# A recurrent attention block and a mixture of experts on one core: the value products of one sequence ahead of those of the other

## The chip, the core and the metric

The kernel runs on one core of a Trainium2 chip. A core has a matrix engine (TensorE, "PE" in the profile, with its weight loads as "PEld"), three engines for element-wise work (VectorE "DVE", ScalarE "ACT", GpSimd "POOL"), a queue for transfers (SyncE, "SP") and 16 DMA engines. Each engine works through its own queue in order, and engines wait for one another by semaphores. TensorE writes its products into PSUM, a memory of eight banks, from which VectorE and ScalarE read. The metric is the device time in microseconds of one execution, as the median of several.

## The reference

Two blocks follow one another. The first is a gated linear recurrence over 768 steps for 4 sequences with 8 heads of width 48; the second sends each of the 3072 rows to one of 16 experts, chosen in two levels.

```python
f = 1.0 / (1.0 + np.exp(-f_logit))                    # (B, H, S, D) = (4, 8, 768, 48)
for t in range(S):
    state = f[:, :, t, :, None] * state + np.einsum('bhd,bhe->bhde', k[:, :, t], v[:, :, t])
    y[:, :, t] = np.einsum('bhd,bhde->bhe', q[:, :, t], state)
x = np.ascontiguousarray(y.transpose(0, 2, 1, 3)).reshape(B * S, H * D)     # (3072, 384)
...
g_idx = np.argmax(x @ w_group, axis=1)                # one of 4 groups
for g in range(4):
    xg = x[g_idx == g]
    e_idx = np.argmax(xg @ w_expert[g], axis=1)       # one of 4 experts of the group
    for e in range(4):
        h = np.maximum(xg[mask_e] @ w1[g, e], 0.0)    # (rows, 1024)
        out[tok_idx] = combined[:, None] * (h @ w2[g, e])
```

`combined` is the product of the two softmax weights of the chosen group and expert.

## The kernel before

**Units.** The recurrence is computed in chunks of 128 steps. There are 6 chunks `c` and 2 pairs `s` of sequences, so 12 units, numbered 0 to 11, with `units[i] = (c, s)`. A unit holds 128 steps of two sequences (`b` = 0 and 1) with 8 heads each; heads are taken two by two, as `a` (0 to 3) and `r` or `h` (0, 1).

**Within a chunk** the result is a product of masked scores with the values, plus a product of the state before the chunk with the queries. A unit passes through these steps, each a generator that an order advances from one `yield` to the next:

- `bounded` (`c`, line 581, VectorE) and `gated` (`g`, lines 591 to 607): the gate's logarithm (Exp and Ln on ScalarE), its sums over the steps (line 600, TensorE), and two exponentials into `eq` and `kh` (ScalarE).
- `multiplied` (`m`, lines 620 and 623, VectorE) and `turned` (`t`, lines 634 and 635): queries and keys are scaled and then transposed into `Tq` and `Tk`.
- `scored` (`s`): for each `b` 16 products on TensorE (line 660) write scores into two banks `ap`, one for each `r`; VectorE multiplies both with the triangle `tri` and leaves the masked scores in `am[b][:, r]` (line 663). So there are four such mask instructions in a unit, in the order (b=0, r=0), (0, 1), (1, 0), (1, 1).
- `weighed` (`w`): two banks `ys[0]` and `ys[1]`, one for each sequence. The first step adds the products with the old state (line 698, left out in chunk 0), the second the products of the values with the masked scores (line 702), 16 of them with 64 columns of weights. `CORNERS` is `[(0, 0), (0, 1), (1, 0), (1, 1)]`, pairs of `b` and `h`: the head within the pair is `b ^ h`, and `h` says which half of the bank's partitions is written. Then ScalarE copies each bank into `xT[:, b]` (line 705).
- `stated` (`n`, lines 677 to 686): the next state, left out in the last chunk, and with it its 16 products (line 677).
- `done` (`d`): the router's logits from `xT` (line 718), turned by line 723 and summed by line 724. After the second pair of a chunk the chunk's routing (`routed`, `r`) is put in line.
- `listed` (`x`): `xT` is transposed back into rows (line 743), copied by ScalarE (lines 745 and 748), and the rows are kept (units 0 to 7, sent later by SP, line 759) or written to `x_dram` at once (line 751, from POOL in units 8 and 9, from ScalarE's queue in 10 and 11).
- `decayed` (`b`, lines 644 and 645): the chunk's decay.

Each product of 32-bit numbers is two records in the profile, one for each of its two passes, except for transposes, which are one.

**What sets the order.** The order on TensorE, VectorE, ScalarE and SP is the order in which the program issues the instructions; only POOL's is left to the planner. It is written out by hand as lists of steps; a number behind a letter is an offset to the unit:

```python
EVEN = "l+2 d-2 n-1 r r r x-1 x-1 t t t t g+1 g+1 x-1 r s s s s c+2 w d-1 g+2 w g+2 n m+1 m+1".split()
ODD = "l+2 d-2 r r x-1 x-1 t t t t b n-1 g+1 g+1 x-1 r s s s s c+2 w d-1 g+2 w g+2 n m+1 m+1 r n".split()
```

So TensorE's queue around the change is, unit by unit: scores (660), old state (698), logits of the unit before (718), **values with masked scores (702)**, next state (677), logits of an earlier unit turned (723), rows (743), transposes (634), gate sums (600). VectorE's is: four masks (663), bound (581), scaling (620, 623), then routing. ScalarE's is: logits copied (720), Exp (591), the two copies to `xT` (705), Ln (594), rows (745, 748), transposes (635). Units 0 to 2 have an order of their own (`BEGIN`), where `w1 w1` of unit 1 is followed by `d0 x1 x1`; so have the last three.

**Routing.** `route` (lines 178 to 256) finds each row's expert and its place there, and writes weight and number of the row as `meta` to `x_dram` (line 246, POOL). When chunk 3 (`CLOSE`) has been counted, `load_early` ranks the experts on VectorE (lines 271 to 289) and SP starts to load the weights of the two largest (line 381). When its routing ends, `choose_early` names their first 128 rows each (line 318), and `early` gathers these from `x_dram` (line 393, POOL, tile `xg` by `rows_e`), transposes them (line 429), and runs both expert layers (lines 439 and 460) between the last steps of the recurrence; the steps of `early` are the `e` in

```python
NU: "d-2 r e d-1 x-1 x-1 d-1 x-1 r r r e e r e r r e r r e r e r r e e e e e".split(),
```

**Experts.** After the recurrence, passes over the 16 experts follow: a gather of rows (393), the first layer (439) with Relu (440), the second layer (475 or 460), a transpose, the row's weight, and a scatter into the output (450). Weights are loaded by SP three passes ahead.

Of the kernel before, what the change touches and what calls it, by code (L numbers as in the profile page):

```python
# [23 lines left out]
def kernel(  # L24
# [21 lines left out]
    HP = H // 2  # L46
# [33 lines left out]
    def bank(shape, name):  # L80
        return ps.tile(shape, FP32, tag="bank", name=name)
# [437 lines left out]
    with ExitStack() as fast:  # L519
# [29 lines left out]
        CORNERS = [(b, h) for b in range(2) for h in range(2)]  # L549
# [139 lines left out]
        def weighed(i):  # L689

            c, s = units[i]
            w = live[i]
            ys = [bank([P, HP, P], f"y{b}") for b in range(2)]
            if c:
                for a in range(HP):
                    for b, h in CORNERS:
                        rows = slice(DP * (b ^ h), DP * (b ^ h) + D)
                        nc.tensor.matmul(ys[b][DP * h:DP * h + DP, a, :], lhsT=states[s][c % 2][rows, b, a, :], rhs=w["Tq"][rows, b, a, :], start=(a == 0), stop=False, skip_group_check=True)  # L698
            yield
            for a in range(HP):  # L700
                for b, h in CORNERS:
                    nc.tensor.matmul(ys[b][DP * h:DP * h + DP, a, :], lhsT=w["v"][:, b, 2 * a + (b ^ h), :], rhs=w["am"][b][:, b ^ h, a, :], start=(c == 0 and a == 0), stop=True, skip_group_check=True)  # L702
            w["xT"] = xT = sb.tile([P, 2, HP, P], FP32, tag="xT", name="xT")
            for b in range(2):
                nc.scalar.copy(xT[:, b], ys[b])  # L705
            yield
# [73 lines left out]
        def advance(gens):  # L780
# [6 lines left out]


        STAGES = {"c": bounded, "g": gated, "m": multiplied, "t": turned, "s": scored, "n": stated, "w": weighed, "d": done, "x": listed, "b": decayed}
        BEGIN = """c0 h g0 p g0 g0 m0 m0 m0 m0 l2 t0 t0 t0 t0 c1 g1 g1 s0 s0 s0 s0 g1 g1 p w0 w0 n0 m1 m1 m1 m1 l3 h x0 x0 x0  # L790
            t1 t1 t1 t1 b1 c2 g2 g2 s1 s1 s1 s1 p d0 g2 g2 n0 n1 w1 w1 m2 m2 l4 n1
# [274 lines left out]
```

## Time and profile before

| | us |
|---|---|
| median of 5 runs | 418.03 (417.65 to 418.88) |
| the profiled execution | 418.04 |
| its span, first instruction to last | 416.2 |
| TensorE busy | 404.4 (97% of the span) |
| weight loads busy | 375.1 |
| VectorE busy | 267.1 |
| ScalarE busy | 157.3 |
| POOL busy | 83.2 |
| line 702's matmuls, 384 records | 25.1 |
| line 663's masks, 48 instructions | 29.8 |
| line 705's copies, 24 instructions | 12.9 |

The recurrence fills the first 140 us of the span, the experts the rest. The first bursts of line 702 in the 12 units start at 15.01, 25.87, 35.97, 46.96, 57.53, 68.62, 79.19, 90.28, 100.84, 111.95, 124.02 and 133.19 us.

How the profile's lines are read. In the page's second part the span is cut into 40 slices of 10.4 us, and a digit is the busy share in tenths (9 is 90% or more). A line of a group gives line number, engine, operation, output and inputs, shapes and count, then busy time in us, the mean of one in ns, and the engine's idle time just before with what ended it. A line of the timeline gives start and length in us, engine, line, operation, names, shapes and the count of instructions merged into it; in brackets stands the idle time before it, and what ended it. Matmuls are pipelined and their ends are modelled, so a record is longer than the distance to the next.

### The profile page before, as it was taken

To read this page: it belongs to the slowest core of one execution; us is meant where nothing else is said; L and a number is where in the kernel's file an instruction comes from. 1 tells how busy PE (TensorE), PEld (TensorE's weight loads), DVE (VectorE), ACT (ScalarE), POOL (GpSimd) and SP (SyncE) were. 2 spreads that over 40 slices of the span, in tenths; PEclk is the share of its full clock that TensorE was granted. 3 is DMA by queue.
4 is the path that set the end of the run, shared out by engine and by line. 5 is a ranking of instruction groups with operands and counts; after the bars stand their busy time and mean duration, and the time that the engine had idled before them with its cause. 6 is when DMAs were issued, how large, how long until landed. Compare 5 with 4: busy or idle time off the path is not lost.

```text
span 416.2 us, 10080 instructions
## 1 busy us (share of the span) xinstructions
PE 404.4 (97%) x4055; PEld 375.1 (90%) x4055; DVE 267.1 (64%) x778; ACT 157.3 (38%) x353; POOL 83.2 (20%) x127
## 2 busy tenths in 40 slices
PE   5999999999999999999999999999999999999995
PEld 3888888888788878989999999999999999999992
DVE  5666787878898731540799777495595595594240
ACT  5777766666564421211122121232231231231220
POOL 4000010101012047001041321311322321120230
PEclk9999999999999999999999999999999999999999
DMA  9999976778999639985729477495595695595010
GB/s 173 211 194 221 194 151 138 150 149 154 268 332 393 229 131 354 384 289 206 253 100 324 132 261 248 158 331 186 195 349 145 243 330 191 200 321 162 28 47 24
DMA packets 132121, 88.98 MB, mean 214 GB/s; under 512 B 102630, under 2 KB 122700, under 8 KB 132066
## 3 DMA queue, kind: packets, MB, share of 16 engines
q1 hardware_dynamic: 125666, 75.50, 61.8%
q0 software_dynamic: 5792, 11.92, 9.3%
q10 hardware_dynamic: 608, 0.83, 0.6%
q8 instruction: 34, 0.56, 0.6%
q14 instruction: 21, 0.17, 0.1%
HBM read 78.71 MB, written 9.83 MB: 213 GB/s over the span
## 4 chain that ended last, share of the span: by engine, by line
PE 48%; issue 29%; DMA 9%; POOL 6%; DVE 3%; ACT 2%; POOLq 1%
PE hp L439 12%; DMA out_dram<-yt,xg 7%; PE yo L475 6%; PE y L702 5%; PE ap L660 4%; PE cs L600 4%; PE yo L460 4%; POOL out_dram L450 4%; POOL xg L393 2%; PE x_ps L743 2%; PE tr_q L634 2%; PE ds L677 2%; PE tr_k L634 2%; DMA xg<-x_dram,rows_e 2%; PE y L698 2%
## 5 line engine op out<-in xcount | busy, mean ns | idle before, releaser
L439 PE MATMUL hp<-xe,w 128*128 128x128 f32 (+14 forms) x864 | 138.6, 320 | 0.0
L439 PEld LDWEIGHTS hp<-xe,w 128*128 128x128 f32 x864 | 135.8, 190 | 0.8
L475 PE MATMUL yo<-h,w 128*128 128x230 f32 (+13 forms) x672 | 115.8, 333 | 0.0
L422 DVE STREAM_TRANSPOSE yr<-yT 32x192 f32<-32x192 f32 (+1 forms) x208 | 70.5, 339 | 70.4 <-ACT yT L476 67.8
L475 PEld LDWEIGHTS yo<-h,w 128*128 128x128 f32 x672 | 113.7, 190 | 0.2
L415 DVE STREAM_TRANSPOSE xe<-xg 32x192 f32<-32x192 f32 (+1 forms) x208 | 69.7, 335 | 8.6 <-PE hp L439 5.6
L440 ACT ACTIVATE h<-hp 128x256 f32<-128x256 f32 (+14 forms) x72 | 34.4, 478 | 103.5 <-PE hp L439 103.5
L450 POOL DMA_INDIRECT out_dram<-yt,xg x32 | 34.4, 1075 | 149.1 <-ACT yt L447 143.6
L476 ACT COPY yT<-yo 128x230 f32<-128x230 f32 (+13 forms) x42 | 13.5, 326 | 80.5 <-PE yo L475 80.5
L393 POOL DMA_INDIRECT xg<-x_dram,rows_p x30 | 29.6, 988 | 52.7 <-DMA out_dram<-yt,xg 30.0
L663 DVE TENSOR_TENSOR am<-ap,tri 128x512 f32<-128x512 f32 x48 | 29.8, 683 | 12.2 <-PE ap L660 12.2
L702 PE MATMUL y<-am,v 128*64 128x128 f32 x384 | 25.1, 278 | 0.8 <-DVE am L663 0.8
L702 PEld LDWEIGHTS y<-am,v 128*64 128x64 f32 x384 | 20.9, 136 | 4.7 <-DVE am L663 1.9
L660 PE MATMUL ap<-Tq,Tk 48*64 48x128 f32 x768 | 23.8, 272 | 0.2 <-ACT Tk L635 0.2
L660 PEld LDWEIGHTS ap<-Tq,Tk 48*64 48x64 f32 x768 | 20.8, 133 | 2.1 <-issue 1.1
L460 PE MATMUL yo<-w,h 128*128 128x384 f32 x64 | 21.3, 486 | 0.0
L600 PE MATMUL cs<-ld_f,tri 128*128 128x384 f32 x48 | 19.7, 536 | 0.7 <-ACT ld_f L594 0.6
L460 PEld LDWEIGHTS yo<-w,h 128*128 128x128 f32 x64 | 11.9, 190 | 7.4
L607 POOL DMA_DIRECT2D ends<-eq x10 | 5.4, 542 | 57.0 <-ACT eq L601 57.0
L447 ACT ACTIVATE yt<-yr,xg 128x384 f32<-128x384 f32 (+13 forms) x26 | 14.4, 604 | 5.4 <-DVE yr L422 5.4
L705 ACT COPY xT<-y 128x512 f32<-128x512 f32 x24 | 12.9, 589 | 8.6 <-PE y L702 8.6
L634 PE MATMUL tr_q<-ident,qh 128*128 128x128 f32 x96 | 14.9, 278 | 0.3 <-DVE qh L620 0.3
(171 smaller groups left out, 366.3 us busy)
## 6 DMA issues: line engine op xcount, KB each, us to landing
w<-in_moe_w_dram SPq DMA_DIRECT2D x34, 1536.0 KB, 10.8
qh<-in_q_dram SPq DMA_DIRECT2D x12, 384.0 KB, 5.1
ld_k<-in_k_dram SPq DMA_DIRECT2D x12, 384.0 KB, 6.0
v<-in_v_dram SPq DMA_DIRECT2D x12, 384.0 KB, 5.6
ld_f<-in_f_logit_dram SPq DMA_DIRECT2D x11, 384.0 KB, 5.5
x_dram<-x_kept SPq DMA_DIRECT2D x2, 1536.0 KB, 10.9
x_dram<-x POOLq DMA_DIRECT2D x2, 384.0 KB, 7.4
x_dram<-x ACTq DMA_DIRECT2D x2, 384.0 KB, 8.3
```

What stands on the lines that cost most here:

```text
L393: nc.gpsimd.indirect_dma_start(out=w["x"][:, j, :], out_offset=None, in_=x_dram[0:1 + top, :], in_offset=bass.IndirectOffsetOnAxis(ap=rows ...
L415: squares(w, lambda n, k_, rk, g, rg: nc.vector.transpose(out=xT[rg, 0:n, k_], in_=x[rk, 0:n, g]))
L422: squares(w, lambda n, k_, rk, g, rg: nc.vector.transpose(out=y[rk, 0:n, g], in_=yT[rg, 0:n, k_]))
L439: nc.tensor.matmul(hp[:, o, :], lhsT=w1[:, ko, (f + o) * P:(f + o + 1) * P], rhs=w["xT"][:, ko, :], start=(ko == 0), stop=(ko == KO - 1))
L440: nc.scalar.activation(h[:, f:f + 2, :], hp, AF.Relu)
L450: sent = nc.gpsimd.indirect_dma_start(out=out, out_offset=bass.IndirectOffsetOnAxis(ap=w["x"][0:m, j, DM + 1:RW].bitcast(U32), axis=0), in ...
L460: nc.tensor.matmul(yp, lhsT=w["h"][:, fo, :], rhs=w2[:, fo, :], start=(fo == 0), stop=(fo == FO - 1))
L475: nc.tensor.matmul(yp, lhsT=w2[:, fo, m * P:(m + 1) * P], rhs=w["h"][:, fo, :], start=(fo == 0), stop=(fo == FO - 1))
L600: nc.tensor.matmul(cs.rearrange("t h d -> t (h d)"), lhsT=tri, rhs=nl[:, b], start=True, stop=True)
L634: nc.tensor.transpose(out=pt[:, a, :], in_=w[nm + "h"][:, b, 2 * a:2 * a + 2, :].rearrange("t r d -> t (r d)"), identity=ident)
L660: nc.tensor.matmul(ap[r][half, a, :], lhsT=w["Tk"][rows, b, a, half], rhs=w["Tq"][rows, b, a, :], start=True, stop=True)
L702: nc.tensor.matmul(ys[b][DP * h:DP * h + DP, a, :], lhsT=w["v"][:, b, 2 * a + (b ^ h), :], rhs=w["am"][b][:, b ^ h, a, :], start=(c == 0 a ...
```

## The change

Within the second step of `weighed` the 16 products of values with masked scores are issued in another order. Before, the loop over the head pairs `a` is outside and the four corners (sequence `b`, half `h`) are inside, so that products of both sequences alternate by twos. After, the loop over `b` is outside: the eight products of the first sequence come first, then the eight of the second. Within a sequence the order of `a` and `h` is as before, and so are operands, outputs, flags and the number of instructions.

```diff
             yield
-            for a in range(HP):
-                for b, h in CORNERS:
+            for b in range(2):
+                for a, h in [(a, h) for a in range(HP) for h in range(2)]:
                     nc.tensor.matmul(ys[b][DP * h:DP * h + DP, a, :], lhsT=w["v"][:, b, 2 * a + (b ^ h), :], rhs=w["am"][b][:, b ^ h, a, :], start=(c == 0 and a == 0), stop=True, skip_group_check=True)
             w["xT"] = xT = sb.tile([P, 2, HP, P], FP32, tag="xT", name="xT")
             for b in range(2):
                 nc.scalar.copy(xT[:, b], ys[b])
```

The loop over the old state in the step before (line 698) keeps its order.

## The prediction

> **What bounds the kernel.** I read the page's row of slices first, then the groups of line 702, then the timeline around each of its twelve bursts, and last the work that ends the wait at 136 us.
>
> ```profile
> PE   5999999999999999999999999999999999999995
> DMA  9999976778999639985729477495595695595010
> ...
> L702 PE MATMUL y<-am,v 128*64 128x128 f32 x384 | 25.1, 278 | 0.8 <-DVE am L663 0.8
> L702 PEld LDWEIGHTS y<-am,v 128*64 128x64 f32 x384 | 20.9, 136 | 4.7 <-DVE am L663 1.9
> ```
>
> TensorE is busy in every slice but the first and the last, so a microsecond that it loses anywhere between is a microsecond of the end, unless something else is later still. Line 702 shows only 0.8 us of idle time. But the end of a matmul is modelled, and a matmul's record (278 ns) outlasts the step to the next one, so short halts hide in "busy". They show as the length of a burst of 32 (each of the 16 products of a unit is two records):
>
> ```profile
> 35.97 1.97 PE L702 MATMUL y<-am,v 128*64 128x128 f32 x32
> 46.96 2.07 PE L702 MATMUL y<-am,v 128*64 128x128 f32 x32
> 90.28 2.07 PE L702 MATMUL y<-am,v 128*64 128x128 f32 x32
> ...
> 89.87 0.68 DVE L663 TENSOR_TENSOR am<-ap,tri 128x512 f32<-128x512 f32 x1
> ```
>
> The bursts of units 0 and 2 last 1.97, that of unit 1 1.93; those of units 3 to 8 and 10 last 2.07 each, unit 11's 2.22. The fourth mask of unit 7 ends at 89.87 + 0.68 = 90.55, 0.27 after its burst began; in the old order the third product already needs it. So seven units lose 0.10 us each there. Unit 9 loses far more:
>
> ```profile
> 107.61 0.56 DVE L684 TENSOR_TENSOR st<-sp,decays 128x384 f32<-128x384 f32 x1 [1.15 <-ACT decays L645]
> ...
> 110.99 2.46 DVE L663 TENSOR_TENSOR am<-ap,tri 128x512 f32<-128x512 f32 x4
> ...
> 111.95 0.80 PE L702 MATMUL y<-am,v 128*64 128x128 f32 x4
> 113.51 1.75 PE L702 MATMUL y<-am,v 128*64 128x128 f32 x28 [0.76 <-DVE am L663]
> ```
>
> Here VectorE is late, since it ranks the experts (lines 271 to 289) ahead of the masks: four records run, then 28 wait for the mask that ends at 113.45.
>
> A second cost of the old order is on ScalarE. Both banks fill together, so both copies of line 705 start when the whole burst is over, and where no states follow (units 1, 10 and 11) the transposes of line 743 wait for them:
>
> ```profile
> 27.63 1.07 ACT L705 COPY xT<-y 128x512 f32<-128x512 f32 x2 [1.63 <-PE y L702]
> 27.73 0.33 PE L723 MATMUL lg<-ident,lgT 128*128 128x128 f32 x1
> 28.27 1.14 PE L743 MATMUL x_ps<-ident,xT 128*128 128x128 f32 x8 [0.21 <-ACT xT L705]
> ...
> 82.11 0.33 PE L723 MATMUL lg<-ident,lgT 128*128 128x128 f32 x1
> 82.27 1.04 PE L743 MATMUL x_ps<-ident,xT 128*128 128x128 f32 x8
> ...
> 126.56 1.15 PE L743 MATMUL x_ps<-ident,xT 128*128 128x128 f32 x8 [0.21 <-ACT xT L705]
> ```
>
> At 82 us (unit 6, with line 677's work between) the same steps need 0.16 us from line 723 to line 743, and 1.04 for the eight. At 27.73 it is 0.54 and 1.14.
>
> **The change, part by part.** It adds and removes no instruction, no DMA and no tile. It reorders 16 products in TensorE's own queue; the orders of ScalarE, VectorE and SP stay as written, and nothing moves past SP's or POOL's issues. Sums are against the profiled execution: 418.04 us, a span of 416.2 and 1.8 around it. The median of the five runs is 418.03, so they are one.
>
> (a) *Masks of the second sequence are needed later.* Eight products of the first come ahead: half of 1.97 less the last record's tail of 0.27, so some 0.9 us after the burst's start (an estimate). The fourth mask is there after 0.27, some 0.6 to spare. Units 3 to 8 and 10 fall to unit 2's 1.97: 0.10 each, 0.60 by unit 8. Unit 11's 2.22 is left as it is, since its masks end at 133.12, before its burst at 133.19; a gain there would go into (e) anyhow.
>
> (b) *Unit 9.* Its 12 remaining records of the first sequence run while the last masks are made, and only 16 stay behind 113.51. At (1.75 - 0.27) / 27 = 0.055 from one to the next, the burst ends 12 x 0.055 = 0.65 sooner against VectorE.
>
> (c) *The first copy of line 705 starts about 0.9 us sooner*, and the second at the burst's end. Where ScalarE idles (1.63 ahead of 27.63, 1.50 ahead of 125.92) the transposes no longer wait: unit 1 gains 0.54 - 0.16 = 0.38 and 1.14 - 1.04 = 0.10, together 0.47 with the third digits; unit 10 likewise 0.48. The second copy ends at 27.63 + 0.59 = 28.22, and the fifth transpose would want it at 27.89 + 0.44 = 28.33, so the cover is 0.1 us; if that is gone, 0.1 of each gain is. Elsewhere the first copy still queues behind the Exp of line 591 and the transposes come after line 677's 1.09 us, so it brings nothing.
>
> (d) *One more handing-over per unit* (ScalarE is released at the 16th record too). Line 743 hands its first bank over after four of eight: 1.04 for eight and 0.60 for the four of line 634 at 83.14, (1.04 - 0.60) / 4 = 0.11 a step, and 0.11 within the four as well ((0.60 - 0.27) / 3). I take nothing. The Trainium skill, TensorE: Matmul & The Clock Gate, "The cost: per-tile semaphore tail", speaks against the change here: it counts 26.3 ns for each further increment that matmuls make. By it 12 units would pay 0.32 us, and the forecast would be 416.9; the steps of line 743 show no such cost.
>
> (e) *What is late next.* Loads don't hold it: the keys whose issue begins at 31.98 land a median 6.0 us later and are first used at 48.48. So TensorE, ScalarE and VectorE move by 0.47 + 0.60 = 1.07 up to unit 9, TensorE by 1.72 behind it, and by 1.72 + 0.10 + 0.48 = 2.30 at line 723 of 135.35. But there it must wait for a gather:
>
> ```profile
> 118.18 0.73 POOL L751 DMA_DIRECT2D x_dram<-x  x1 [11.59 <-ACT x L748]
> 120.90 0.76 POOL L246 DMA_DIRECT2D x_dram<-meta  x1 [1.80 <-DVE number L293]
> 128.99 1.06 POOL L393 DMA_INDIRECT xg<-x_dram,rows_e  x1 [7.33 <-DVE full L304]
> ...
> 135.35 0.33 PE L723 MATMUL lg<-ident,lgT 128*128 128x128 f32 x1
> 136.12 0.52 PE L429 MATMUL xg_ps<-ident,xg 128*128 128x128 f32 x3 [0.44 <-DMA xg<-x_dram,rows_e]
> ```
>
> Line 304 had ended at 128.84, but POOL's own queue shows it waiting on transfers until 128.17: the meta write of 120.90, which took 7.2 us to land, behind the x write of 118.18 in POOL's queue. The meta write follows VectorE, which has no idle time but 0.17 us from 107.6 to 122, so its issue moves by 1.07 only; the x write follows unit 9's transposes and moves by 1.72. The landing moves by something between. I take the middle, 1.4. The gather and line 429 follow it, TensorE waits 0.9 us more there, and all behind (hp, yo, the passes' gathers, the last scatter) hangs on TensorE or on routing that starts after line 429: 1.4 is what is left at the end. Sum: 418.04 - 1.4 = 416.6; bounds 418.04 - 1.72 = 416.3 and 418.04 - 1.07 = 417.0.
>
> **The rivals.**
>
> *The gather doesn't move.* The DMA row is at 9 from 104 to 135 us, and the x write of line 751 takes 5.1 us to land at best and 9.8 at worst. If bulk traffic sets the landing, all 2.3 us go into the wait at 136.12, and it is 418.0. Against it: the bulk (kept rows, expert weights) is issued behind the same engines and starts 1.07 sooner.
>
> *More gets through.* Without the x write just ahead of it the meta write needs less than 7.2 us, and the gather less than 7.0. To pass TensorE's whole 2.30 both together must lose 1.2: 415.7. For it: the largest of the x writes' times is in this very crush. Against: nothing leaves it.
>
> *Slower: runs into one bank.* Eight pairs in a row now write one bank, where the bank changed after every two. That is 3 more successions a sequence, 72 in all. If each costs the 0.10 that a halt costs now, it is 7.2 - 1.4 = 5.8 us more, 423.8. It decides from 1.4 / 72 = 0.02 us each. Against it: line 677 puts 32 records of the same shape of weights into the one bank of ds in 1.09 us, (1.09 - 0.22) / 31 = 0.028 a record, and line 718 16 into lT in 0.64. For it: neither has 128 columns to a record and two column groups at once, as line 702 does.
>
> **How the numbers follow.** Forecast 0.61, the gather stays 0.14, more gets through 0.11, slower 0.14. Its own range is 416.3 to 417.0. From 415.8 to 418.0 it takes in most of the second rival and, with a little scatter, most of the first; the slower case and what is left of these two is 2 in 10. A difference of 0.2% (0.84 us) is about what a measurement of this kernel can tell from none. The forecast and the second rival lie beyond it: 0.72 faster, 0.14 same, 0.14 slower.
>
> **What would show it.** In the profile after: bursts of line 702 at 1.97 in units 3 to 8 and 10; unit 9's idle time for am inside the burst down from 1.0 us to under 0.5; the first copy of line 705 in units 1 and 10 some 0.9 us ahead of the second, and line 743 without idle time; unit 8's burst at about 99.9 (100.84 - 0.47 - 5 x 0.10) in place of 100.84; line 429's wait for the gather up from 0.44 to over 1 us. I am wrong if bursts stay at 2.07, if they grow past it, or if line 429 starts as late as 136.1.

## The result, and the profile after

| | before | after |
|---|---|---|
| median, us | 418.29 (417.65 to 419.73, 60 runs) | 417.70 (416.39 to 418.66, 36 runs) |
| ratio to before, 95% interval | | 0.9985 [0.998, 0.999] |
| the profiled execution, its span | 418.04, 416.2 | 416.21, 414.4 |

The change gains 0.6 us, where 1.4 was forecast. The profiled execution of after is no typical one: at 416.21 us it is below all 36 timed runs. What it shows up to unit 10 recurs in other executions of this kernel, but for single halts; a line 429 as early as in it does not, and the experiments are about this difference.

The page's slices and groups of line 702 after:

```profile
PE   5999999999999999999999999999999999999995
DMA  9999997877999559984828467586496595585010
...
L702 PE MATMUL y<-am,v 128*64 128x128 f32 x384 | 24.4, 276 | 0.1
L702 PEld LDWEIGHTS y<-am,v 128*64 128x64 f32 x384 | 21.0, 137 | 3.2 <-issue 1.8
```

The group lost 0.7 us of "busy" and its 0.8 us of idle time for `am`. The timeline of after shows where, in units 2, 3, 7 and 9:

```profile
35.63 1.97 PE L702 MATMUL y<-am,v 128*64 128x128 f32 x32
46.62 1.97 PE L702 MATMUL y<-am,v 128*64 128x128 f32 x32
89.51 1.97 PE L702 MATMUL y<-am,v 128*64 128x128 f32 x32
...
110.01 2.46 DVE L663 TENSOR_TENSOR am<-ap,tri 128x512 f32<-128x512 f32 x4
...
110.97 2.65 PE L702 MATMUL y<-am,v 128*64 128x128 f32 x32
...
118.09 0.29 PE L251 MATMUL tb<-val,ln 128*128 128x64 bf16 x4 [0.67 <-DVE val L233]
```

Bursts are 1.97 in units 3 to 8 and 10, as they were in units 0 and 2. Unit 9's burst is one of 2.65 where it took from 111.95 to 115.26. The wait in the last line is new. Before, line 251 started without idle time:

```profile
119.07 0.29 PE L251 MATMUL tb<-val,ln 128*128 128x64 bf16 x4
```

Now TensorE has gained 0.65 us on VectorE in unit 9, and waits 0.67 for it at line 251.

Units 1 and 10, and the road to line 429, in the same timeline of after:

```profile
26.90 0.58 ACT L705 COPY xT<-y 128x512 f32<-128x512 f32 x1 [0.97 <-PE y L702]
27.77 0.58 ACT L705 COPY xT<-y 128x512 f32<-128x512 f32 x1 [0.29 <-PE y L702]
27.66 0.33 PE L723 MATMUL lg<-ident,lgT 128*128 128x128 f32 x1
27.82 1.25 PE L743 MATMUL x_ps<-ident,xT 128*128 128x128 f32 x8
...
116.62 0.73 POOL L751 DMA_DIRECT2D x_dram<-x  x1 [11.01 <-ACT x L748]
119.92 0.76 POOL L246 DMA_DIRECT2D x_dram<-meta  x1 [2.37 <-DVE number L293]
127.04 1.06 POOL L393 DMA_INDIRECT xg<-x_dram,rows_e  x1 [6.37 <-DVE oh L195]
...
133.93 0.33 PE L723 MATMUL lg<-ident,lgT 128*128 128x128 f32 x1
134.11 0.52 PE L429 MATMUL xg_ps<-ident,xg 128*128 128x128 f32 x3
```

Line 743 now starts 0.16 after line 723, as forecast, but its eight take 1.25 where they took 1.14 (1.04 was forecast): the second copy starts at 27.77, and the fifth transpose waits for it. And line 429 starts at 134.11 without any idle time, 2.01 us sooner than before. Forecast was a wait of over 1 us. In this execution the meta write landed after 6.27 us (7.23 before), so TensorE and the gather met.

From burst to burst, after against before: unit 1 gives 0.27 (10.10 to 9.84); units 3 to 8 give 0.10 to 0.12 each, 0.64 together; unit 9 gives 0.65 and loses it again at line 251; unit 10 gives 0.37 (9.17 to 8.80), 0.10 of it in its burst; unit 11's burst gives 0.06. That is 1.34, and with a first burst 0.08 sooner 1.42 at line 723, of the 2.30 forecast.

### The profile page after: what moved, and what is told of

It reads as the page before. It is cut to its first block, busy times and chain, and to the rows that moved or that the text cites. A ratio compares the mean times of both kernels' runs of the same rounds, so it can differ in the third digit from the quotient of the medians.

```text
span 414.4 us, 10083 instructions
## 1 busy us (share of the span) xinstructions
PE 403.2 (97%) x4055; PEld 375.2 (91%) x4055; DVE 267.0 (64%) x778; ACT 156.8 (38%) x353; POOL 83.2 (20%) x127
## 4 chain that ended last, share of the span: by engine, by line
PE 50%; issue 29%; DMA 7%; POOL 6%; DVE 3%; ACT 2%; POOLq 1%
PE hp L439 12%; DMA out_dram<-yt,xg 7%; PE yo L475 7%; PE y L702 5%; PE ap L660 5%; PE cs L600 4%; PE yo L460 4%; POOL out_dram L450 4%; PE x_ps L743 2%; POOL xg L393 2%; PE tr_q L634 2%; PE ds L677 2%; PE tr_k L634 2%; PE y L698 2%; PE lT L718 2%
```

## The experiments

Two explanations of the missing microsecond were set against one another. In the first, the **gather** (called G in the later expectations), line 429 starts when its rows land, whenever TensorE is ready. In the second, **halts** (F), TensorE stands still for parts of a microsecond inside its bursts, waiting for nothing that the trace names, while its own instructions are being fetched.

The experiments ran on four chips, the kernel before beside them on each. On three its median is 424.7 to 425.0, on the one of the wide scores below 419.08. So a run is compared with runs on its own chip, and the kernel before was also run again under names of its own (`old` and so on). Such a repeat came out at 1.0000, 0.9987 and 0.9983 of the kernel before, so that a difference of less than some 0.2% between two runs says little. The 0.15% of the result is itself no larger. The ratios are not exactly quotients of the medians given beside them; the two can differ by 0.1%.

### Both kernels again, and line 429 later

`again` is the changed kernel and `old` the kernel before, unchanged. In `late_new` and `late_old` the first `e` of the step order, line 429 with its wait, is moved behind line 743; they stand on the new and on the old order of products.

```diff
-            NU: "d-2 r e d-1 x-1 x-1 d-1 x-1 r r r e e r e r r e r r e r e r r e e e e e".split(),
+            NU: "d-2 r d-1 x-1 x-1 d-1 x-1 r e r r e e r e r r e r r e r e r r e e e e e".split(),
```

> The changed kernel, nothing else edited, for a second trace and a second timing. The profiled execution of the change had a span 1.8 us under that of before, while its median is only 0.6 us under. Theory A (the gather of the early experts' rows lands when the transfers let it): the bursts of line 702 start where they did in the first trace, unit 10's at 123.0 to 123.1 us, and the difference in span between the two traces, 1.0 us or more if this execution is a usual one, arises at the first transposes of line 429, which start between 134.1 and 135.8. Theory B (the gain is lost elsewhere: at the start, or in the experts' passes): line 429 starts at 134.1 as before and the difference arises ahead of 120 us or behind 160 us. Ratio near 0.9985 in both.

> The kernel before, nothing edited: how far two timings and two traces of one kernel differ. Ratio 1.000 within 0.001. Theory A: bursts of line 702 at the same times as in its first trace within 0.1 us, unit 10's at 124.0; line 429's first transposes anywhere between 135.4 (no wait) and 136.8. Theory B: the traces differ ahead of 120 us or behind 160 us by as much as the times do.

> The changed order with the first early expert's transposes (line 429) moved behind the last unit's rows (line 743), so that TensorE has some 1.5 us of other work before it needs the gather. Theory A: the wait for the gather goes or shrinks to the rest, and against before the time falls by 1.5 to 2.3 us (ratio 0.9945 to 0.9965), well under the changed kernel's 0.9985. Theory B: no more than 0.2 us below the changed kernel, ratio 0.998 to 0.999.

> The old order of line 702 with the same move of line 429. In the old order TensorE waits 0.4 to 0.7 us for the gather. Theory A: 0.3 to 0.7 us faster than before (ratio 0.9983 to 0.9993), and the distance from this to the changed order with the move is 1.2 us or more. Theory B: the distance between the two with the move is the same 0.6 us as without it.

Measured: `again` 424.10 us, 0.9987 [0.9965, 1.001]; `old` 424.42, 1.0 [0.9977, 1.0022]; `late_new` 424.63, 1.0003 [0.998, 1.0026]; `late_old` 424.49, 0.9995 [0.9968, 1.0023]. The first explanation had expected 0.9945 to 0.9965 for `late_new`, which lies outside its interval. Otherwise times tell nothing apart here. The traces do: from the first burst to unit 10's it is 109.04 (`old`) and 109.02 (`late_old`) in the old order, 108.10 in `late_new`, and 108.94 in `again`, which has a halt of 0.83 inside unit 6's burst. Work put ahead of the wait did not make the end sooner, so these times do not speak for the gather. But the end is 6 us later on this chip than in the first profiles, and the place where it is lost is elsewhere. In `old`, where the passes over the experts begin:

```profile
168.18 0.57 PE L439 MATMUL hp<-xe,w 128*128 128x128 f32 x3 [0.30 <-issue]
169.58 0.51 PE L439 MATMUL hp<-xe,w 128*128 128x128 f32 x3 [0.82 <-issue]
171.01 0.27 PE L439 MATMUL hp<-xe,w 128*128 128x128 f32 x1 [0.93 <-issue]
172.10 6.12 PE L439 MATMUL hp<-xe,w 128*128 128x230 f32 x15 [0.82 <-DVE xe L430]
```

Idle time with "issue" was ended by nothing that the profile names. From the passes' first product (line 439, near 160 us) to the first of their second layer it is 22.0 us here and 15.3 in the profiles of before and after; from there to the end 240.1 and 240.2. So most of what this span is longer by (6.7 of 8.4 us) is lost at this one place, in both orders, and on these chips it differs from execution to execution (19.0 to 22.0). That makes the intervals wide; the last section comes back to it.

### The new order in unit 9 alone

```diff
-            for a in range(HP):
-                for b, h in CORNERS:
+            for a, b, h in [(a, b, h) for b in range(2) for a in range(HP) for h in range(2)] if i == 9 else [(a, b, h) for a in range(HP) for b, h in CORNERS]:
```

> The new order in unit 9 alone, the old one in the other eleven. Forecast on record: 0.65 us sooner behind unit 9, and kept by TensorE at least up to 135 us. Theory V: VectorE has no idle time from 107 to 122 us, so line 251, which needs VectorE's val (line 233), waits 0.65 us and gives it all back before unit 10's scores: unit 9's burst from first to last start 2.38 us in place of 3.04, but unit 10's burst at the same distance from unit 8's as before (23.18 us, within 0.05), and ratio 1.000 within 0.001.

Measured: 424.98 us, 0.9998 [0.9973, 1.0022]. From the first burst to unit 10's: 109.07, as in the old order. The timeline of this run from 110 us on (line 702 is 701 in it), and then the waits of TensorE (us in total, times, longest):

```profile
112.70 2.66 PE L701 MATMUL y<-am,v 128*64 128x128 f32 x32
```

```profile
PE tb L251 <- DVE val L233: 0.7, 1, 0.7
```

Unit 9's burst shrinks as forecast, and line 251 takes all of it back. What unit 9 gains is VectorE's time, and VectorE has no more of it to give.

### Loads held back from the gather

SP's loads of the second expert layer for the two early experts start right behind those of the first, and so fill the DMA engines while the gather runs. `held_new` and `held_old` issue them only at unit 11's masks.

```diff
-            w1s, w2s = ([load_layer(wp, e, layer) for e in es] for layer in (1, 2))
-            weights.update(enumerate(zip(w1s, w2s)))
+            w1s.extend(load_layer(wp, e, 1) for e in es)
+
+        def load_second():
+            nc.vector.tensor_copy(who_late, who[:, 0:EARLY])
+            es = [value(who_late[0:1, p:p + 1], GE - 1) for p in range(EARLY)]
+            weights.update(enumerate(zip(w1s, [load_layer(wp, e, 2) for e in es])))
...
-            NU - 1: "d-2 r r n-1 x-1 x-1 t t t t r x-1 r s s s s w b d-1 w r r".split(),
+            NU - 1: "d-2 r r n-1 x-1 x-1 t t t t r x-1 r s s s s y w b d-1 w r r".split(),
```

> The changed kernel once more, nothing edited. In the first four runs the bursts of line 702 up to unit 10 kept their distances to within 0.1 us in every trace of one order (but for one halt of 0.83 us inside a burst), while TensorE stood still, with nothing that it waited for ('issue'), within the scores of unit 11 (line 660, 1.0 to 1.5 us) and at 162 to 176 us (line 439, 3.6 to 6.7 us). Theory F: while the DMA engines are full TensorE runs out of instructions, since these are fetched by DMA too, and such halts swallow or add a varying part of the time. Then this trace differs from the first one of the change by halts with 'issue' at lines 660 and 439, and by less than 0.3 us anywhere else between 20 and 127 us. Theory G: only the gather for line 429 varies. Then the whole difference arises at line 429. Ratio 0.997 to 1.000.

> The old order of line 702, with the loads of the two early experts' second layers (3.1 MB) held back on SP until unit 11's masks are made, by a copy of the experts' numbers at that place on VectorE. So the DMA engines have less to do from about 128 to 136 us. Theory F: unit 11's scores (line 660) last 1.71 us with no halt, and unit 11's burst starts 9.0 to 9.2 us behind unit 10's, on whichever chip; the gather for line 429 takes under 6.5 us to land. Theory G: the halts in line 660 stay, only the gather is sooner. In time between 1 us faster and 1 us slower than before, since the second layers' weights may now come late for line 460 (150 us).

> The changed order with the same loads held back. Theory F: no halt in unit 11, and against the run with the old order and the loads held back the whole gain of TensorE up to there stays: line 723 of unit 11 is 1.3 to 1.7 us sooner, and the time 1.0 to 1.7 us shorter unless halts at 162 to 176 us hide it. Theory G: 0.6 us as without holding back.

Measured: `again2` 423.73 us, 0.9990 [0.9972, 1.0009]; `held_old` 424.01, 0.9987 [0.9969, 1.0004]; `held_new` 423.03, 0.9958 [0.9941, 0.9976]. The gather for line 429 takes 4.7 (`held_old`) and 5.0 us (`held_new`) from issue to landing, against 6.7 to 7.1 in the nine profiles of the kernels before and after. So these loads have a large part in how long it takes.

Neither explanation is borne out whole. `again2` is as F expected: it reaches unit 10's burst after 108.09 us, the first profile of after in 108.11, and behind that it has halts in lines 660 and 439. With the loads held back F expected no halt in unit 11, its burst 9.0 to 9.2 us behind unit 10's, and line 723 sooner by 1.3 to 1.7 in the new order. The burst is 9.07 behind in `held_old` but 10.25 in `held_new`, which has halts of up to 0.36 in line 660, and line 723 is 0.15 sooner. The medians of the two differ by 0.98 us, between G's 0.6 and F's 1.0 to 1.7.

### Fewer instructions on TensorE

In `wide_old` and `wide_new` a score product takes 128 columns of weights at once where it took two halves of 64: 384 matmuls and 384 weight loads fewer, in the old and in the new order of line 702.

```diff
-                        for u in range(2):
-                            half = slice(u * P // 2, (u + 1) * P // 2)
-                            nc.tensor.matmul(ap[r][half, a, :], lhsT=w["Tk"][rows, b, a, half], rhs=w["Tq"][rows, b, a, :], start=True, stop=True)
+                        nc.tensor.matmul(ap[r][:, a, :], lhsT=w["Tk"][rows, b, a, :], rhs=w["Tq"][rows, b, a, :], start=True, stop=True)
```

> The old order of line 702, with the scores of line 660 not split into two halves of 64 columns: 8 products with 128 columns of weights a sequence in place of 16 with 64, so 64 matmuls and weight loads fewer a unit and pass pair, the same result. Theory F (TensorE runs out of instructions in units 10 and 11 and at the start of the experts, since their fetch is late behind the bulk transfers): with half the instructions in line 660 the scores take the same 1.7 us by the array, and the halts in unit 11's scores (1.0 to 1.5 us in seven of the traces so far) go; unit 11's burst starts 9.0 to 9.3 us behind unit 10's. Theory G (the halts have to do with the transfers of operands, not of instructions): they stay at 1 us or more. If two halves in parallel are what makes line 660 fast, it takes 3.4 us and the kernel is 20 us slower: then it tells nothing.

> The same with the new order of line 702. Theory F: no halt in unit 11 (8.7 to 8.9 us from unit 10's burst to unit 11's), and line 429 1.2 to 2.0 us sooner, from unit 0's burst on, than with the old order and wide scores. Theory G: halts of 1 us or more at line 660, and 0.6 us.

> The changed kernel, for another trace. From the first burst of line 702 to that of unit 10 108.1 us within 0.05 unless a halt with 'issue' falls in; from there to line 429 11.1 us without halts and 12.3 to 13.0 with them. If this is a chip on which the kernel before takes 418 us, theory F expects a typical execution (within 0.4 us of the median) to have such halts of 0.5 to 1.5 us between 127 and 137 us, and theory G a later gather instead: line 723 to line 429 0.5 us or more, without halts.

> The kernel before, for another trace: 109.0 us from the first burst to unit 10's; from there to line 429 12.1 us as in its first trace, where the wait for the gather swallows halts of up to 0.7 us, and more with larger ones. Ratio 1.000 within 0.001.

Measured, on the chip like the first: `wide_old` 419.41 us, 1.0008 [0.9997, 1.0019]; `wide_new` 418.65, 0.9984 [0.9974, 0.9993]; `again3` 417.92, 0.9968 [0.9955, 0.998]; `old2` 418.42, 0.9987 [0.9975, 0.9998]. New against old order on this chip, by the medians: 0.50 us as it is, 0.76 with wide scores. The wide scores themselves cost more than they save: 110.35 and 110.08 to unit 10's burst.

In the wide runs line 429 waits for nothing, since its rows have landed 0.99 and 1.23 us ahead of it. From the first burst to line 723 it is 121.55 in the old order and 121.02 in the new, and to the first product of the passes 146.77 and 145.97. So TensorE's lead is 0.80 where the passes begin, and the medians differ by 0.76. The halts in unit 11's scores, which F expected to go, occur on this chip in no order (unit 11's burst comes 9.17 us after unit 10's in `old2` and 8.79 in `again3`), so that this part of F was not tested.

The profiled execution of `again3`, 417.64 us, is the typical one that the first was not. Its timeline:

```profile
78.56 1.31 PE L702 MATMUL y<-am,v 128*64 128x128 f32 x20
80.14 0.88 PE L702 MATMUL y<-am,v 128*64 128x128 f32 x12 [0.27 <-issue]
...
120.45 0.76 POOL L246 DMA_DIRECT2D x_dram<-meta  x1 [2.37 <-DVE number L293]
128.88 1.06 POOL L393 DMA_INDIRECT xg<-x_dram,rows_e  x1 [7.67 <-DVE run L305]
...
133.06 1.75 PE L702 MATMUL y<-am,v 128*64 128x128 f32 x27 [0.15 <-issue]
134.73 0.33 PE L723 MATMUL lg<-ident,lgT 128*128 128x128 f32 x1
135.75 0.52 PE L429 MATMUL xg_ps<-ident,xg 128*128 128x128 f32 x3 [0.69 <-DMA xg<-x_dram,rows_e]
136.20 0.65 PE L718 MATMUL lT<-xT,gw 128*32 128x128 f32 x16
136.77 1.09 PE L743 MATMUL x_ps<-ident,xT 128*128 128x128 f32 x8
```

And that of `old2`, 418.26 us:

```profile
128.64 1.06 POOL L393 DMA_INDIRECT xg<-x_dram,rows_e  x1 [6.91 <-DVE boost L299]
...
134.08 1.69 PE L702 MATMUL y<-am,v 128*64 128x128 f32 x26 [0.16 <-issue]
135.70 0.33 PE L723 MATMUL lg<-ident,lgT 128*128 128x128 f32 x1
135.59 1.07 ACT L705 COPY xT<-y 128x512 f32<-128x512 f32 x2 [1.91 <-PE y L702]
135.86 0.49 PE L429 MATMUL xg_ps<-ident,xg 128*128 128x128 f32 x3
136.28 1.07 PE L718 MATMUL lT<-xT,gw 128*32 128x128 f32 x16
137.28 1.09 PE L743 MATMUL x_ps<-ident,xT 128*128 128x128 f32 x8
```

TensorE is 0.97 us sooner at line 723 in the new order, and line 429 starts only 0.11 sooner: the gather's POOL instruction started at 128.88 against 128.64. In the old order a halt inside unit 11's burst cost some 0.1 us, since line 429 starts 0.26 us behind the landing there and never less than 0.14; in the new order the gather is what is left. Both have halts of about 0.5 us in that burst; with wide scores it has none in either order (1.695 us from first to last start).

But line 429 is not the end of the story. Line 718 behind it reads both copies of line 705. In `old2` the second copy ends at 136.66, while line 718 is already at work, and its 16 records take 1.07 us; in `again3` the copies are ready, and they take 0.65. So line 743 comes 0.51 us sooner in `again3`, and its span is 0.56 us shorter. This gain of unit 11 is in no sum of the prediction, which had the wait for the gather cover it.

The queues of the DMA view speak for what halts are. First `again3`, then `wide_new`; columns are packets, megabytes and share of 16 engines:

```profile
q8 instruction: 34, 0.56, 0.6%
```

```profile
q8 instruction: 31, 0.51, 0.5%
```

Three blocks of 16,384 bytes fewer for 768 TensorE instructions fewer is 64 bytes for each, so by these numbers the queue carries TensorE's program. The blocks come at about 125, 131 and 139 us, while the DMA engines are full (share 1.03 from 125 to 137 us in `again3`), and the halt in unit 11's burst of `again3`, at 132.9, follows a block that starts at 130.7 and takes 1.0. So it is with all six single halts of 0.15 us and more inside line 702's bursts (unit 9's waits aside): they end 1.2 to 1.5 us after a block has landed, the four in unit 6 at a DMA share of 0.6 to 0.8 in the 3 us before. But in lines 660 and 439 on the other chips halts recur for as long as 6 and 23 us after the last block, and TensorE works between them, so that it then had instructions. That late blocks cause the halts was not shown.

### Everything once more

`old3`, `again4`, `held_old2` and `held_new2` are the kernels of these names without the last digit, unchanged.

> The kernel before, word for word, as the yardstick of this call. Both theories: ratio 1.000 within 0.0015, which is the scatter that two submissions of one kernel showed (old 1.0000, old2 0.9987). The gather lands 120.6 to 121 us after the first burst less 0.2, and line 723 to line 429 takes 0.2 to 0.8 us.

> The changed kernel, word for word. Theory G (TensorE gains 1.3 us up to line 723, and the landing of the first gather, which hardly moves, swallows what exceeds 0.6): from the first burst to line 429 within 0.5 us of old3, wait from line 723 to line 429 about 1 us, ratio 0.997 to 0.999. Theory F (halts of TensorE while blocks of instructions arrive swallow it): halts inside bursts of 0.5 us or more, no wait for the gather, the same ratio. Rival (nothing swallows it, the first profile of after is the usual execution): 0.9965 or less.

> Old order, the loads for the early experts' second layer held back on SP until unit 11's masks. Theory G: the gather needs 5 us in place of 7 to land, so TensorE no longer waits for it and the 0.2 to 0.8 us between line 723 and line 429 falls to 0.17; ratio 0.998 to 0.9995 (held_old was 0.9987). Theory F: as old3, 1.000.

> New order with the same hold. Theory G: with the gather out of the way the whole gain of TensorE shows: 1.2 us against held_old2, ratio 0.9955 to 0.997 to the kernel before, and below again4. Theory F: halts stay, so the same as again4 within 0.0005. held_new was 0.9958 [0.9941, 0.9976] in an earlier call.

Measured: `old3` 424.23 us, 0.9983 [0.9957, 1.0008]; `again4` 424.08, 0.9993 [0.9966, 1.002]; `held_old2` 423.69, 0.9966 [0.9942, 0.9989]; `held_new2` 422.91, 0.9955 [0.993, 0.998]. By the medians the new order gains 0.15 us as it is (by the ratios it loses 0.1%) and 0.78 with the loads held back, after 0.32 and 0.98 in the earlier runs on such chips (`again` with `old`, `held_new` with `held_old`). Each ratio is uncertain by some 0.25%, 1 us, so that this does not tell the explanations apart. Both explanations missed signs. `again4` reached line 429 0.81 us sooner than `old3`, where G had them within 0.5, and took 0.34 from line 723 to line 429, where G had about 1. None of its bursts of line 702 has the halt of 0.5 us that F expected; its halts ahead of line 429 are in unit 11's scores, with unit 11's burst 10.54 us behind unit 10's. And `held_old2` was faster than either had said.

Much of the scatter on these chips goes with the clock that was granted to TensorE, which is on record for every run: on each of the three a mean clock lower by 0.001 goes with 0.43 to 0.45 us more (an estimate, by a straight line through all runs on the chip). At equal clock the new order gains, with 95% intervals, 0.46 ± 0.59 (`again`) and 0.58 ± 0.51 (`again4`) where line 429 follows the gather, and 1.05 ± 0.64 (`late_new`), 0.81 ± 0.42 (`held_new`) and 0.72 ± 0.50 (`held_new2`) where it does not, each against the old order on its chip. All point one way; that the gain is larger without the gather in the way is not shown.

`held_new2` no longer waits for the gather:

```profile
128.47 1.06 POOL L393 DMA_INDIRECT xg<-x_dram,rows_e  x1 [7.79 <-DVE pick L211]
...
130.50 0.45 PE L660 MATMUL ap<-Tq,Tk 48*64 48x128 f32 x5 [0.26 <-issue]
131.24 0.34 PE L660 MATMUL ap<-Tq,Tk 48*64 48x128 f32 x3 [0.30 <-issue]
...
135.31 0.33 PE L723 MATMUL lg<-ident,lgT 128*128 128x128 f32 x1
135.47 0.49 PE L429 MATMUL xg_ps<-ident,xg 128*128 128x128 f32 x3
```

Its gather landed at 132.83, and halts in unit 11's scores (line 660) took its place: unit 11's burst came 10.37 us after unit 10's, against 8.8 in the first profile of after. So here, with the gather out of the way, TensorE lost time to halts.

### What the nine profiles say together

Times from the first burst of line 702, in us, for the kernels that differ in nothing but the order:

| run | to unit 10's burst | meta issued | meta landed | gather landed | line 723 | line 429 | line 429 after landing |
|---|---|---|---|---|---|---|---|
| before | 109.01 | 105.90 | 113.13 | 120.97 | 120.34 | 121.11 | 0.14 |
| old2 | 109.01 | 105.89 | 112.70 | 120.52 | 120.61 | 120.78 | 0.26 |
| old | 109.04 | 105.92 | 113.65 | 121.62 | 121.59 | 121.76 | 0.14 |
| old3 | 109.31 | 106.19 | 113.72 | 121.51 | 121.67 | 121.84 | 0.32 |
| after | 108.11 | 104.99 | 111.26 | 119.04 | 119.00 | 119.18 | 0.14 |
| again3 | 108.60 | 105.48 | 113.05 | 120.64 | 119.76 | 120.78 | 0.14 |
| again | 108.94 | 105.82 | 113.99 | 121.84 | 121.46 | 121.97 | 0.14 |
| again2 | 108.09 | 104.98 | 112.62 | 120.39 | 120.32 | 120.52 | 0.14 |
| again4 | 108.25 | 105.13 | 113.03 | 120.89 | 120.69 | 121.03 | 0.14 |

In the new order line 429 starts 0.14 after the landing in all five executions: the gather ends last each time, if often only just. In the old order it does so in two of four. How long TensorE stood there is another matter. From line 723 to line 429 it takes 0.17 without a wait; it took 0.77, 0.17, 0.17 and 0.16 in the old order and 0.18, 1.02, 0.51, 0.20 and 0.34 in the new.

What the landing hangs on is the same in all 18 profiles: the meta write starts 0.19 us after VectorE's line 293, and the gather's POOL instruction 0.85 to 0.86 us after that write has landed, whichever line of VectorE the timeline names. The meta write is issued 0.69 sooner on average (105.97 to 105.28), needs 7.51 us instead of 7.33 and so lands 0.51 sooner. The rows land 0.59 sooner (a mean of 121.15 to 120.56), TensorE reaches line 723 0.81 and line 429 0.67 sooner. Landings of the new order lie up to 2.8 us apart, so the 0.59 is uncertain by some 0.5 (its standard error), and that it equals the gain of the medians says little.

## Why the prediction was off

**(a) Masks needed later: right**, in place and size. Bursts of 1.97 in units 3 to 8 and 10; the undisturbed executions gain the 0.10 of each.

**(b) Unit 9: right at its place, wrong as a gain.** The 0.65 arrived and went back at line 251, which waits for VectorE's line 233. The working asked what is late next only at line 429; a wait some 4 us behind the burst, on the same VectorE, had no idle time in the trace of before and so did not show. That VectorE has no idle time to spare from 107.6 to 122 us the prediction itself says, but it used this for the meta write alone. `only9` shows it by itself.

**(c) The first copy: half.** Copies now start 0.87 us apart, and line 743 no longer waits for the first. But "the second copy starts at the burst's end" was mis-sized: it starts 0.32 us after the last record's start (27.455 to 27.77, 124.73 to 125.05), not about 0.1, as it seemed in the old order, where the first bank's last record lay two pairs ahead of the burst's end. The cover of 0.1 was gone, and unit 1 gave 0.27 for 0.47, unit 10's end 0.27 for 0.48. Unit 11, which was left out, has a gain of the same kind wherever line 429 does not wait (line 718 in `old2` and `again3`).

**(d) One more hand-over: nothing, as taken, but there was none to cost anything.** By the semaphore updates in the traces line 702's burst hands over twice in either order, at its 28th and 32nd record before and at its 16th and 32nd after. From unit 0's burst to unit 1's it is 10.86 before and 10.87 after. The rule of the Trainium skill (TensorE: Matmul & The Clock Gate, "The cost: per-tile semaphore tail") charges each increment, so that it makes nothing of this change, and no run here tests it.

**(e) is the step that failed.** "The landing moves by something between. I take the middle, 1.4": the end moved by 0.6 (0.4 to 0.8 by the interval), below the lower bound of 1.07. Both bounds were distances by which an issue moves, and the step gave the transfers the same length as before. The clearest comparison is that of `before` and `again3`, where TensorE waits for the rows in both. The rows land 0.33 sooner (120.97 to 120.64), and the span is 0.40 shorter. The meta write was issued 0.42 sooner, since (c) gave half and a halt in unit 6 took 0.49; it took 0.34 longer to land, and the gather 0.26 less. Over the nine profiles the landing moves by the 0.59 above. The meta write's issue moved by 0.9 at most, and less where a halt lay ahead of it (0.83 in unit 6 of `again`), and its way through full DMA engines took between 6.3 and 8.2 us whatever the order.

The 2.30 at line 723 failed as well. It was 1.34 in the profile of after, which lost (b) and half of (c), and 0.81 on average, with halts. That the landing decides when line 429 starts was right in all five profiles of the new order; that the wait there grows to over 1 us was right in `again3` alone, and mostly TensorE and the rows came within 0.4 us of one another. How much of the medians' loss is the landing's and how much that of (b), (c) and the halts was not shown.

Of the rivals, "the gather doesn't move" came close in one pair: in `again3` against `old2` it landed 0.13 later, counted from the first burst. Over all profiles it moved by 0.59. "More gets through" is what the one profiled execution of after did, 416.21 us by a meta write that landed after 6.27 us; it was no rule. "Runs into one bank" is refuted: bursts of eight pairs in one bank take the 1.695 us from first to last start that the alternating ones took in units 0 and 2. The profile of after by itself would nearly have confirmed the forecast (416.21, just below its range of 416.3 to 417.0), and only the median of many runs and a second profile of the same kernel spoke against it.

What stays open: why TensorE halts, and whether the new order is worth TensorE's whole 1.3 us once the gather is out of the way and nothing halts. Single profiles of these kernels on the chips with over 424 us differ by up to 3.4 us behind line 429, nearly all of it in the pass of the last section. The best ratios are those of `held_new` and `held_new2` (0.9958 [0.9941, 0.9976] and 0.9955 [0.993, 0.998]); against the changed kernel on the same chips they are 0.7 and 1.2 us shorter. They ran only on chips where the kernel before takes over 424 us.

## What to carry to other kernels

When a transfer ends last at a meeting of engines, a gain on the engine is worth what the landing moves, and a landing behind full DMA engines need not move as far as its issue (0.33 here, where the issue moved 0.42 and 1.07 was the forecast's lower bound): take no movement as the lower bound, not the issues of the engines. Check by the traces' semaphore updates what an order really hands over. Follow a gain to every later wait on the engine that was late, also to waits that have no idle time yet. And profile the changed kernel twice, and set both against the median, before believing in either trace.

## What was not expected of the hardware

On three chips TensorE halts within line 439 at 164 to 172 us, in all twelve profiles, and in ten of them the granted clock then falls. The stretches of `again4` (us, busy time and instructions of PE, PEld, DVE, ACT and POOL, clock, DMA share, GB/s):

```profile
160.00:164.00 4.00, 4.00 (x32) 3.60 (x31) 0.00 (x0) 0.58 (x1) 3.01 (x4) 1.00 1.03 349
164.00:168.00 4.00, 2.79 (x23) 2.37 (x21) 0.00 (x0) 0.38 (x1) 2.95 (x3) 1.00 1.03 367
168.00:172.00 4.00, 2.58 (x10) 2.26 (x11) 2.45 (x7) 0.94 (x3) 0.00 (x0) 0.83 1.02 397
172.00:176.00 4.00, 4.00 (x17) 3.67 (x17) 3.85 (x12) 0.55 (x1) 0.00 (x0) 0.74 1.06 397
```

Busy time falls first, with the DMA share at 1.03, and the clock falls behind it. The means of 0.83 and 0.74 come from one stretch at 0.50, from 170.6 to 174.1 us, while TensorE is busy again from 170.5. Such a stretch lasts 3.41 us in seven profiles and 6.83 in three (`old`, `held_old`, `held_old2`). The pass takes 20.2 to 20.7 us with the one, 21.7 to 22.0 with the other, 19.0 in `again2` and `late_old`, with halts and the clock at 1.00, and 15.3 in the first profiles, without halts. The Trainium skill (TensorE: Matmul & The Clock Gate, "What's actually happening") has a gate that follows TensorE's activity in windows of some 3.4 us, and the order of events and the length of the stretch agree with it, though no single idle time here was longer than 1.9 us (`held_old`).
